# Attention, feed-forward and mixture of experts on one core: decays as float32r parts, q and k of the first pair loaded first, denser warm-up

## The chip, the core and the metric

The kernel runs on one core of one Trainium2 chip. Its engines have instruction queues of their own: TensorE (PE; its weight loads are shown apart as PEld), VectorE (DVE), ScalarE (ACT), GpSimd (POOL) and SyncE (SP, which here only issues DMAs). Each works through its queue in program order and waits on semaphores of the others. The metric is the device time of one execution in microseconds.

## The reference

Three stages follow one another, all in float32, on 2304 tokens of width 512:

```
cum = cumsum(log(clip(f, 1e-4, 1)))                    # 4 batches x 8 heads x 576
scores = q k^T / 8 + cum[i] - cum[j], causal           # "forget" attention, head size 64
attn = softmax(scores);  x = attn v                    # reshaped to 2304 x 512
h = x w_in;  g = h if h>=1, 0 if h<=-1, else (h+1)^2/4
x = g w_out                                            # 512 -> 2048 -> 512
e = argmax(normalise(x) . normalise(emb));  gate = softmax prob of e
out = gate * relu(x w1[e]) w2[e]                       # 8 experts, 512 -> 1024 -> 512
```

## The kernel before

**Attention.** The 32 heads are worked through as 16 pairs (i = 0 to 15; four pairs make a batch). Per pair, `load` fetches q and k (`rawq`, `rawk`, four DMAs each), `turned` transposes them on VectorE (`qt`, `kt`), and five units follow, c = 4, 3, 2, 1, 0: c = 4 takes the last 64 rows of both heads (576 columns, as two matmuls of 288), c < 4 a block of 128 rows against w = 128(c+1) columns for each head. A unit's scores go into one of two double banks of PSUM (`SR`, `SRx`); VectorE subtracts the mask and takes the row's extreme (L548), ScalarE takes the exponential and its sum (L553), VectorE the reciprocal (L558, L560), GpSimd scales (L564), TensorE transposes the probabilities (L578) and multiplies them with v (`X`, L618; `U`, L671).

**The decays.** `forget_rows` loads f four times, one under the other, on 4 x 32 rows, and turns it into `cum`, -8 times the running sum of the logarithms (L348 to L353). For pairs 4 to 15, the row of each head is written to memory and loaded back spread over all partitions (`cm`, `cl`), and VectorE subtracts it with the mask. For pairs 0 to 3 (`NSUM` = 4), which come before that could be there, TensorE adds it into the bank instead: `sums` multiplies a selecting column of `ident` (or a block of `pick`) with `cum`, in float32 (L514, L520). For c < 4 the two heads' sums read rows 0 to 31 and 64 to 95.

**Weights.** The kernel's wide matrix products take float32 operands as two float32r parts (high and low). Weights lie in memory as 8-byte numbers. Pieces of 128 x 512 are loaded into `war` and put together in `wax` by ScalarE and VectorE (L790 to L797), rounded to the high part on ScalarE (L801), and the low part is the difference, on GpSimd (L802). Half of the feed-forward layer's hidden columns (`half0`: 16 pieces `wa`, products `hp` and `accp`) is done between the pairs of the attention, from pair 4 on; the other half (`wb`, `hr`, `accr`) and the experts follow.

**Order.** The order on each engine is written out ahead by a planner in the kernel, the class `Order`: every step is a generator that asks for an engine with an estimated duration and a priority, and whoever is ready in the planner's time with the best priority is issued next. Loads of weights have due times in that time (`FIRST_WEIGHTS`). `keep_warm` gives TensorE small matmuls `warm` of the identity where the planner finds nothing else and the planned activity is low (`WARM`).

Of the kernel before, what the change touches and what calls it, by code (L numbers as in the profile page):

```python
# [9 lines left out]
F32 = mybir.dt.float32  # L10
# [14 lines left out]
def f32(ap):  # L25
    return ap.bitcast(F32)
# [11 lines left out]
NQK = 3  # L38
NP_ = 8
NSUM = 4  # L40
FIRST_WEIGHTS = [2000.0 + 2800.0 * n for n in range(6)] + [20000.0 + 5500.0 * n for n in range(10)]
WARM_FROM, WARM = 3000.0, 0.45


class Event:
# [149 lines left out]
def act(n, fn, prio=5.0, more=0.0):  # L195
    return Use("ACT", 155 + n / 1.2 + more, fn, prio)
# [27 lines left out]
def kernel(  # L224
# [65 lines left out]
    qz = [ap.tile([P, P], F32, name=f"qz{n}") for n in range(NQK)]  # L290

    cum = ap.tile([P, S], F32, name="cum")
    low = ap.tile([P, S], F32, name="low")
    pick = ap.tile([NH, P * NSUM], F32, name="pick")
    past = [ap.tile([P, n], F32, name=f"past{n}") for n in (512, S)]

    SR = [psa.tile([P, 2, 512], F32, name="SR"), psf.tile([P, 2, 512], F32, tag="acc", name="SRx")]
# [25 lines left out]
    def setup():  # L323
        make_identity(nc, ident)
        nc.vector.tensor_copy(pick.rearrange("p (h q) -> p h q", q=64),
                              ident[:NH, :2 * NSUM].unsqueeze(2).to_broadcast([NH, 2 * NSUM, 64]))
        for t in qz:
            nc.gpsimd.memset(t, 0.0)
        for t in past:
            nc.gpsimd.memset(t, 0.0)  # L330
        w = past[0][:, 384:]
        nc.gpsimd.affine_select(out=w, in_=w, pattern=[[-1, P]], compare_op=ALU.is_ge,
                                fill=-8e9, base=0, channel_multiplier=1)
        for j in range(2):
            w = past[1][64 * j:64 * j + 64, 512:]
            nc.gpsimd.affine_select(out=w, in_=w, pattern=[[-1, 64]], compare_op=ALU.is_ge,
                                    fill=-8e9, base=0, channel_multiplier=1)

    def forget_rows():


        def loads():
            for p0 in range(0, P, NH):
                nc.scalar.dma_start(cum[p0:p0 + NH], f.rearrange("b h s -> (b h) s"))
        yield Use("DVE", 400, lambda: (nc.vector.memset(quarter, 0.25), nc.vector.memset(low, -8.0)), 0)
        yield dma(4 * NH * S * 4, loads, 0, "ACT", k=4)
        yield Use("ACT", 1400, lambda: nc.scalar.activation(tiny, quarter, AF.Ln), 0)
        yield dve(S, lambda: nc.vector.tensor_scalar(cum, cum, 1e-4, 1.0, ALU.max, ALU.min), 0, True)  # L348
        yield act(S, lambda: nc.scalar.activation(cum, cum, AF.Ln), 0)
        go(exp_table())  # L350
        yield dve(S, lambda: nc.vector.tensor_scalar(cum, cum, -8.0, None, ALU.mult), 0, True)

        yield dve(S, lambda: nc.vector.tensor_tensor_scan(cum, low, cum, 0.0, ALU.max, ALU.add), 0)  # L353
        done(sums_there)
        yield dma(NH * S * 4, lambda: nc.sync.dma_start(rows, cum[:NH]), 2)
        done(rows_there)

    def exp_table():
        yield Use("ACT", 1400, lambda: nc.scalar.activation(tiny, quarter, AF.Exp), 0.5)
# [129 lines left out]
    def unit(i, c, started):  # L489

        yield qk_ok[i]
        heads = (None,) if c == 4 else (0, 1)
        gp_ = yield (p_b, len(heads))
        sl = yield (sr_b, ((0, 1), (2, 3)))
        bank = SR[sl[0] // 2]
        done(started)
        (qt, kt), z, _ = qkt[i]
        w = P * (c + 1) if c < 4 else S

        def scores():  # L500
            if c == 4:
                for n in range(2):
                    nc.tensor.matmul(bank[:, n, :S // 2], z, kt[:, S // 2 * n:S // 2 * (n + 1)],  # L503
                                     start=True, stop=i >= NSUM)
                return
            for j in range(2):
                p = slice(64 * j, 64 * j + 64)
                nc.tensor.matmul(bank[:, j, :w], qt[p, P * c:P * c + P], kt[p, :w],  # L508
                                 start=True, stop=i >= NSUM)

        def sums():
            if c == 4:
                for n in range(2):
                    nc.tensor.matmul(bank[:, n, :S // 2], pick[:, P * i:P * i + P],  # L514
                                     cum[:NH, S // 2 * n:S // 2 * (n + 1)], start=False, stop=True)
                return
            for j in range(2):
                p = slice(64 * j, 64 * j + NH)
                h = 64 * j + 2 * i + j
                nc.tensor.matmul(bank[:, j, :w], ident[p, h:h + 1].to_broadcast([NH, P]),  # L520
                                 cum[p, :w], start=False, stop=True)
        yield Use("PE", max(440, 1.72 * w), scores, 0.8, full=0.8)
        done(s_done[i])
        if i < NSUM:
            yield sums_there
            yield Use("PE", max(440, 1.72 * w), sums, 0.8, full=0.8)
        yield cm_ok[i, c]
        st = ap.tile([P, 8], F32, tag="st", name=f"st{i}_{c}", bufs=10)
        summed, scaled = Event(len(heads)), Event()
        left = Event(len(heads))  # L530
        for n, j in enumerate(heads):
            p = ap.tile([P, S], F32, tag="P", name=f"P{i}_{j}{c}", bufs=NP_)
            go(head(i, j, c, p, [gp_[n]], bank, st, summed, scaled, left))
        yield left
        give(sr_b, sl)
# [151 lines left out]
    def keep_warm(until):  # L687

        yield WARM_FROM
        while until.n > 0:  # L690
            g = yield (x_b, 1)
            X = psa.tile([P, 512], F32, tag="X", name=f"warm{o.seq}")
            while not x_b.waiters and until.n > 0:
                if o.slow == 2.0 or o.work < WARM * (o.now - o.window):
                    yield Use("PE", mm(P, 2), lambda: nc.tensor.matmul(
                        X[:, :P], ident, ident, start=True, stop=True), 9, after=0.0)
                else:
                    yield o.now + 150.0
            give(x_b, g)

    def attention():
        go(forget_rows())
        yield Use("POOL", 3000, setup, 0)
        go(keep_warm(xs_ok[0]))
        yield 100.0
        go(prep())
        yield sums_there
        go(loadv(0))
        for i in range(NP):
            if i + 1 < NP:  # L710
# [899 lines left out]
```

## Time and profile before

| | |
|---|---|
| median of three timed runs | 878.93 us (877.66 to 880.08) |
| the profiled execution | 878.33 us |
| its span, first to last instruction | 876.7 us |
| mean granted clock of TensorE | 0.978 |
| busy: PE, DVE, ACT, POOL | 849.6, 456.7, 360.3, 302.2 us |

The span is what the trace covers. Busy time is a sum over stages with different limits: the attention's first pairs stand in the first 80 us or so, its last in about 320, and from then on the wide matrix products fill TensorE. The granted clock is a share of full speed: 1.00 is 2.4 GHz, 0.50 is 1.2 GHz.

### The profile page before, as it was taken

The page shows a single profiled execution, that of the slowest core. Times are in us where ns is not written, and L with a number is a line of the kernel's source. Part 1 is how long each engine was busy: PE and PEld are TensorE (multiplying, and loading weights), DVE is VectorE, ACT ScalarE, POOL GpSimd, SP SyncE. Part 2 cuts the span into 40 slices and gives each one's busy share as a digit, 9 for nine tenths or more (in the row PEclk, how much of TensorE's full clock was granted, in tenths as well). Part 3 has the DMA queues.
Part 4 walks back from the last instruction along what each step waited for, and adds up shares of the span by engine and source line. Part 5 has one row for each costly group of instructions (what it writes and reads, how often), then busy time and mean ns, then how long its engine had stood idle before and what let it go on. Part 6 is the DMA issues. An engine that isn't in the chain of part 4 may idle for free.

```text
span 876.7 us, 14896 instructions
## 1 busy us (share of the span) xinstructions
PE 849.6 (97%) x5300; PEld 687.7 (78%) x5300; DVE 456.7 (52%) x1099; ACT 360.3 (41%) x838; POOL 302.2 (34%) x405
## 2 busy tenths in 40 slices
PE   7999998999999999999899999999999999999994
PEld 4655775787877789999788888888898888887684
DVE  4788778565655536676763445376643522212110
ACT  3477766655656545444533242423333212112010
POOL 2466777454654633444432122322210033000000
PEclk7699998999999999999999999999999999999998
DMA  7987756554522315343521134564431111721210
GB/s 154 143 182 173 184 141 137 127 127 116 141 66 90 93 60 135 100 134 105 196 69 49 73 120 142 162 184 150 157 121 49 49 48 49 267 94 54 92 49 25
DMA packets 153658, 100.89 MB, mean 115 GB/s; under 512 B 102724, under 2 KB 125764, under 8 KB 153584
## 3 DMA queue, kind: packets, MB, share of 16 engines
q1 hardware_dynamic: 150608, 95.43, 39.9%
q0 software_dynamic: 2784, 4.21, 1.8%
q8 instruction: 42, 0.69, 0.3%
q10 hardware_dynamic: 192, 0.30, 0.2%
q14 instruction: 32, 0.26, 0.1%
HBM read 76.33 MB, written 23.84 MB: 114 GB/s over the span
## 4 chain that ended last, share of the span: by engine, by line
PE 88%; DVE 5%; POOL 2%; DMA 2%; ACT 1%; issue 1%; SPq 0%; POOLq 0%; ACTq 0%; DVEq 0%
PE hm L847 12%; PE hr L847 11%; PE hp L847 9%; PE accp L976 8%; PE accm L984 6%; PE accr L976 6%; PE accBr L976 6%; PE accBm L984 5%; PE SR L508 5%; PE X L618 4%; PE T L578 4%; PE SR L503 2%; PE gt L1158 1%; PE U L671 1%; POOL wb L802 1%; DVE wbx L795 1%
## 5 line engine op out<-in xcount | busy, mean ns | idle before, releaser
L869 POOL TENSOR_TENSOR glr<-gr,ghr 128x512 fp32r<-128x512 f32 x36 | 46.7, 1298 | 153.3 <-PE accBr L976 73.7
L564 POOL TENSOR_SCALAR P<-P,st 128x512 f32<-128x512 f32 (+3 forms) x128 | 78.9, 629 | 48.7 <-DVE st L560 26.3
L847 PE MATMUL hr<-rx,wb 128*128 128x512 f32 (+1 forms) x384 | 89.1, 366 | 0.4 <-DVE rx L833 0.4
L847 PE MATMUL hm<-mx,wm 128*128 128x512 f32 (+1 forms) x336 | 87.4, 381 | 0.0
L553 ACT ACTIVATE P<-P,st 128x512 f32<-128x512 f32 (+3 forms) x128 | 71.5, 560 | 36.8 <-DVE st L548 35.4
L976 PE MATMUL accp<-ghp,wa 128*128 128x256 f32 x576 | 83.3, 287 | 3.2 <-DVE x_7b L1005 3.2
L976 PEld LDWEIGHTS accp<-ghp,wa 128*128 128x128 f32 x576 | 73.7, 191 | 6.7 <-DVE x_7b L1005 3.4
L878 DVE SCALAR_TENSOR_TENSOR glm<-hm,ghm 128x512 fp32r<-128x512 f32 x36 | 24.8, 690 | 103.4 <-PE accBm L984 68.6
L847 PEld LDWEIGHTS hr<-rx,wb 128*128 128x128 f32 x384 | 65.7, 188 | 13.2 <-DVE rx L833 0.8
L877 ACT ACTIVATE ghm<-hm 128x512 fp32r<-128x512 f32 x36 | 21.6, 599 | 132.6 <-PE accBm L984 111.3
L847 PEld LDWEIGHTS hm<-mx,wm 128*128 128x128 f32 x336 | 61.0, 188 | 15.7 <-issue 3.4
L869 POOL TENSOR_TENSOR glp<-gp,ghp 128x512 fp32r<-128x512 f32 x36 | 47.8, 1329 | 51.4 <-ACT ghp L868 46.8
L578 PE MATMUL T<-ident,P 128*128 128x128 f32 x320 | 55.6, 293 | 5.4 <-POOL P L564 5.0
L548 DVE CUSTOM_DVE_ANT_0 P<-SR,cm 128x512 f32<-128x512 f32 (+3 forms) x96 | 44.6, 485 | 26.7 <-PE SR L508 24.7
L578 PEld LDWEIGHTS T<-ident,P 128*128 128x128 f32 x320 | 38.2, 147 | 18.5 <-POOL P L564 8.9
L598 ACT COPY pt<-T 128x512 f32<-128x512 f32 (+2 forms) x96 | 34.8, 391 | 39.3 <-PE T L578 39.1
L863 DVE SCALAR_TENSOR_TENSOR gr<-tr 128x512 f32<-128x512 f32 x36 | 25.9, 719 | 45.7 <-POOL glr L869 27.0
L984 PE MATMUL accm<-wm,ghm 128*128 128x512 f32 x160 | 48.9, 395 | 0.0
L859 ACT ACTIVATE tr<-hr,quarter 128x512 f32<-128x512 f32 x36 | 24.8, 688 | 55.3 <-PE hr L847 25.5
L976 PE MATMUL accr<-ghr,wb 128*128 128x512 f32 (+1 forms) x160 | 47.1, 376 | 0.0
L976 PE MATMUL accBr<-ghr,wb 128*128 128x512 f32 (+1 forms) x160 | 46.6, 373 | 0.0
L976 PE MATMUL accp<-glp,wa 128*128 128x256 f32 x288 | 46.3, 283 | 0.2 <-POOL glp L869 0.2
(335 smaller groups left out, 1838.8 us busy)
## 6 DMA issues: line engine op xcount, KB each, us to landing
cm<-rows SPq DMA_DIRECT2D x24, 256.0 KB, 4.5
rawq<-in_q_dram SPq DMA_DIRECT2D x64, 72.0 KB, 3.2
rawk<-in_k_dram SPq DMA_DIRECT2D x64, 72.0 KB, 3.2
xs<-xT SPq DMA_DIRECT2D x16, 288.0 KB, 2.1
x2n<-nat SPq DMA_DIRECT2D x18, 256.0 KB, 2.3
war<-in_moe_w_in_dram SPq DMA_DIRECT2D x8, 512.0 KB, 4.6
war<-in_moe_w_out_dram SPq DMA_DIRECT2D x8, 512.0 KB, 3.5
rawv<-in_v_dram SPq DMA_DIRECT2D x32, 128.0 KB, 2.7
```

The source lines that it names most:

```text
L508: nc.tensor.matmul(bank[:, j, :w], qt[p, P * c:P * c + P], kt[p, :w], start=True, stop=i >= NSUM)
L548: yield dve(w + 80, lambda: nc.vector.tensor_tensor_reduce(out=pv_, in0=so, in1=m, scale=-0.125, scalar=3e38, op0=ALU.add, op1=ALU.min, ac ...
L553: yield act(w, lambda: nc.scalar.activation(pw, pw, AF.Exp, bias=st[:, n:n + 1], scale=-1.0, accum_out=st[:, 2 + n:3 + n]), 1, 330)
L564: yield pool1(w, lambda: nc.gpsimd.tensor_scalar(pw, pw, st[:, 6 + n:7 + n], 1.0, ALU.mult, ALU.mult), 0)
L578: nc.tensor.transpose(T[:, P * n:P * n + P], p[:, P * kb:P * kb + P], ident)
L598: yield act(n, lambda: nc.scalar.copy(dh, src), 0)
L618: nc.tensor.matmul(X[D * j:D * j + D, P * kb:], vt[:, kb, j], pt[i, j][0][:, 512 * kb:512 * kb + 512 - P * kb], start=(kb == 0), stop=(kb ...
L847: nc.tensor.matmul(oo, a[:, c, cs], x[c], start=(ip == 0 and c == 0), stop=(ip == 2 and c == KC - 1))
L863: yield dve(n, lambda: nc.vector.scalar_tensor_tensor(g, t, 0.5, t, ALU.min, ALU.mult), 2)
L869: yield pool2(n, lambda: nc.gpsimd.tensor_tensor(gl, g, f32(gh), ALU.subtract), 1)
L976: nc.tensor.matmul(acc[d][:, :w], b[:, fc, P * d:P * d + P], g, start=(fc == 0 and ip == 0 and (not narrow or d % 2 == 0)), stop=(fc == NF ...
L984: nc.tensor.matmul(acc[a], g[:, P * a:P * a + P], b[:, fc], start=(fc == 0 and ip == 0), stop=(fc == NF - 1 and ip == 2))
```

## The change

Three edits. `cum` is split for pairs 1 to 3 into three float32r parts that lie one under the other on 96 rows of `parts`: its rounding, the rounding of what is left, and the rest (`sum_parts`). The sums of these pairs are then float32r matmuls over 96 rows, with a selecting block `picks` that has the identity three times; pair 0 keeps its float32 sums. The preparation of q and k starts ahead of the setup, and the first weights are due at 6.0 instead of 2.0 us of the planner's time (later ones are moved too). The warm-up matmuls start at 1.5 instead of 3.0 us and are given up to 30 us whenever TensorE has nothing else. The planner's price of the new sums is lower, so the order moves in all engines.

```diff
-FIRST_WEIGHTS = [2000.0 + 2800.0 * n for n in range(6)] + [20000.0 + 5500.0 * n for n in range(10)]
-WARM_FROM, WARM = 3000.0, 0.45
+FIRST_WEIGHTS = [6000.0 + 2700.0 * n for n in range(5)] + [20500.0 + 5200.0 * n for n in range(11)]
+WARM_FROM, WARM = 1500.0, 0.6
...
-    pick = ap.tile([NH, P * NSUM], F32, name="pick")
+    parts = ap.tile([P, S], F32R, name="parts")
+    pick = ap.tile([NH, P], F32, name="pick")
+    picks = ap.tile([P, P * NSUM], F32R, name="picks")
...
     def setup():
...
+        for n in range(3):
+            p = slice(NH * n, NH * n + NH)
+            nc.vector.tensor_copy(
+                picks[p].rearrange("p (h q) -> p h q", q=64),
+                ident[p, NH * n:NH * n + 2 * NSUM].unsqueeze(2).to_broadcast([NH, 2 * NSUM, 64]))
...
     def forget_rows():
+        got = yield (p_b, 3)
+        low, rest, mids = (ap.tile([P, S], F32, tag="P", name=n, bufs=NP_)
+                           for n in ("low", "rest", "mids"))
+        go(sum_parts(rest, mids, got))
...
+    def sum_parts(rest, mids, got):
+        mids = mids.bitcast(F32R)
+        yield sums_there
+        yield act(S, lambda: nc.scalar.copy(parts, cum), 0.9)
+        yield dve(S, lambda: nc.vector.tensor_tensor(rest, cum, f32(parts), ALU.subtract), 0.9)
+        yield act(S, lambda: nc.scalar.copy(mids, rest), 0.9)
+        yield Use("ACT", 700, lambda: nc.scalar.copy(parts[NH:2 * NH], rest[NH:2 * NH]), 0.9)
+        yield dve(S, lambda: nc.vector.tensor_tensor(rest, rest, f32(mids), ALU.subtract), 0.9)
+        yield Use("ACT", 700, lambda: nc.scalar.copy(parts[2 * NH:3 * NH], rest[2 * NH:3 * NH]), 0.9)
+        give(p_b, got)
+        done(parts_there)
...
         def sums():
+            n3 = 3 * NH
+            if i == 0:
...
             if c == 4:
                 for n in range(2):
-                    nc.tensor.matmul(bank[:, n, :S // 2], pick[:, P * i:P * i + P],
-                                     cum[:NH, S // 2 * n:S // 2 * (n + 1)], start=False, stop=True)
+                    nc.tensor.matmul(bank[:, n, :S // 2], picks[:n3, P * i:P * i + P],
+                                     parts[:n3, S // 2 * n:S // 2 * (n + 1)], start=False, stop=True)
                 return
             for j in range(2):
-                p = slice(64 * j, 64 * j + NH)
-                h = 64 * j + 2 * i + j
-                nc.tensor.matmul(bank[:, j, :w], ident[p, h:h + 1].to_broadcast([NH, P]),
-                                 cum[p, :w], start=False, stop=True)
+                h = 64 * (2 * i + j)
+                nc.tensor.matmul(bank[:, j, :w], picks[:n3, h:h + 1].to_broadcast([n3, P]),
+                                 parts[:n3, :w], start=False, stop=True)
...
-            yield sums_there
-            yield Use("PE", max(440, 1.72 * w), sums, 0.8, full=0.8)
+            yield parts_there if i else sums_there
+            yield Use("PE", mm(w if c < 4 else S // 2, 2) if i else 1.72 * w, sums, 0.8)
...
-                if o.slow == 2.0 or o.work < WARM * (o.now - o.window):
+                if o.now < 30000.0 or o.slow == 2.0 or o.work < WARM * (o.now - o.window):
...
     def attention():
         go(forget_rows())
+        go(prep())
         yield Use("POOL", 3000, setup, 0)
         go(keep_warm(xs_ok[0]))
-        yield 100.0
-        go(prep())
```

SyncE's queue at the program's start, before (the first rows):

```order
L781 DMA war<-in_moe_w_in_dram 128x4x128
L370 DMA rawq_135<-in_q_dram 32x18x32 x4
L370 DMA rawk_144<-in_k_dram 32x18x32 x4
L781 DMA war<-in_moe_w_out_dram 128x512
L355 DMA rows<-cum 32x576
```

and of the changed kernel:

```order
L394 DMA rawq_134<-in_q_dram 32x18x32 x4
L394 DMA rawk_143<-in_k_dram 32x18x32 x4
L814 DMA war<-in_moe_w_in_dram 128x4x128
L814 DMA war<-in_moe_w_out_dram 128x512
L367 DMA rows<-cum 32x576
```

The first weights' load has moved from ahead of q to behind k.

VectorE's queue from the first work on the decays to pair 0's first reduction (`P_None`), before:

```order
L348 TENSOR_SCALAR cum<-cum 128x576
L418 STREAM_TRANSPOSE qt_128<-rawq_135 128x576
L791 TENSOR_SCALAR wax<-wax 128x512
L351 TENSOR_SCALAR cum<-cum 128x576
L418 STREAM_TRANSPOSE kt_129<-rawk_144 128x576
L353 SCALAR_TENSOR_TENSOR cum<-low,cum 128x576
L793 TENSOR_SCALAR wax<-wax 128x512
L795 SCALAR_TENSOR_TENSOR wax<-war,wax 128x512
L797 SCALAR_TENSOR_TENSOR wax<-war,wax 128x512
L548 ISA P_None_204,st_4_203<-SR,past_91 128x576
```

and of the changed kernel:

```order
L442 STREAM_TRANSPOSE qt_104<-rawq_134 128x576
L442 STREAM_TRANSPOSE kt_105<-rawk_143 128x576
L360 TENSOR_SCALAR cum<-cum 128x576
L363 TENSOR_SCALAR cum<-cum 128x576
L365 SCALAR_TENSOR_TENSOR cum<-low,cum 128x576
L824 TENSOR_SCALAR wax<-wax 128x512
L826 TENSOR_SCALAR wax<-wax 128x512
L374 TENSOR_TENSOR rest<-cum,parts 128x576
L828 SCALAR_TENSOR_TENSOR wax<-war,wax 128x512
L830 SCALAR_TENSOR_TENSOR wax<-war,wax 128x512
L582 ISA P_None_221,st_4_220<-SR,past_92 128x576
```

The transposes of q and k now stand ahead of the decays, and the first subtract of `sum_parts` (L374) stands ahead of the first reduction.

TensorE's queue from the program's start into pair 0, before:

```order
L695 MATMUL warm_127<-ident 128x128 x19
L503 MATMUL SR<-kt_129,qz_84 128x288 x2
L508 MATMUL SRx<-kt_129,qt_128 128x512 x2
L514 MATMUL SR<-cum,pick 128x288 x2
L520 MATMUL SRx<-cum,ident 128x512 x2
L508 MATMUL SR<-kt_129,qt_128 128x384 x2
L520 MATMUL SR<-cum,ident 128x384 x2
```

and of the changed kernel:

```order
L729 MATMUL warm_148<-ident 128x128 x28
L527 MATMUL SR<-kt_105,qz_84 128x288 x2
L532 MATMUL SRx<-kt_105,qt_104 128x512 x2
L540 MATMUL SR<-cum,pick 128x288 x2
L544 MATMUL SRx<-cum,ident 128x512 x2
L729 MATMUL warm_148<-ident 128x128 x5
L532 MATMUL SR<-kt_105,qt_104 128x384 x2
L729 MATMUL warm_148<-ident 128x128 x2
L544 MATMUL SR<-cum,ident 128x384 x2
```

There are more warm-up matmuls ahead of pair 0's scores, and some stand between its units. Over the whole program `warm` has 88 matmuls instead of 31.

## Rows read from the trace of the kernel before

**Rows 1.** Page of the profile: span, busy shares, granted clock in 40 slices.
```profile
span 876.7 us, 14896 instructions
...
PE 849.6 (97%) x5300; PEld 687.7 (78%) x5300; DVE 456.7 (52%) x1099; ACT 360.3 (41%) x838; POOL 302.2 (34%) x405
```

**Rows 2.** Windows: start, end, length, busy (count) by engine, clock, DMA.
```profile
17.55:35.83 18.28, 17.92 (x81) 10.84 (x79) 12.16 (x42) 10.13 (x28) 7.04 (x12) 0.50 0.85 142
36.47:80.20 43.73, 43.19 (x296) 23.57 (x294) 34.78 (x117) 31.20 (x88) 26.00 (x39) 1.00 0.88 181
40.00:60.00 20.00, 19.77 (x128) 10.11 (x127) 17.39 (x58) 14.86 (x41) 10.44 (x15) 1.00 1.00 172
```

**Rows 3.** Timeline of the start: start us, length, engine, line, work, [idle before].
```profile
0.91 0.45 SPq L781 DMA_DIRECT2D war<-in_moe_w_in_dram  x1
...
1.41 3.03 SPq L370 DMA_DIRECT2D rawq<-in_q_dram  x4
...
1.53 6.45 PE L695 MATMUL warm<-ident 128*128 128x128 f32 x38 [1.53 <-POOL ident masks.py:199]
...
5.77 2.23 SPq L370 DMA_DIRECT2D rawk<-in_k_dram  x4
5.78 0.67 ACT L790 ACTIVATE wax<-war 128x512 f32<-128x512 f32 x1 [1.48 <-DMA war<-in_moe_w_in_dram]
7.81 0.46 DVE L348 TENSOR_SCALAR cum<-cum 128x576 f32<-128x576 f32 x1 [5.16 <-DMA rawq<-in_q_dram]
...
8.31 0.68 ACT L349 ACTIVATE cum<-cum 128x576 f32<-128x576 f32 x1 [1.86 <-DVE cum L348]
...
10.75 0.78 DVE L418 STREAM_TRANSPOSE kt<-rawk 128x576 f32<-128x576 f32 x1 [0.56 <-DMA rawk<-in_k_dram]
11.46 1.32 DVE L353 TENSOR_TENSOR_SCAN cum<-low,cum 128x576 f32<-128x576 f32 x1
...
11.68 1.50 PE L503 MATMUL SR<-kt,qz 128*128 128x288 f32 x4 [3.70 <-DVE kt L418]
...
13.12 0.69 DVE L795 SCALAR_TENSOR_TENSOR wax<-war,wax 128x512 int32<-128x512 int32 x1
...
17.55 0.76 DVE L548 CUSTOM_DVE_ANT_0 P_None<-SR,past 128x576 f32<-128x576 f32 x1 [3.01 <-PE SR L514]
```

**Rows 4.** Windows of 2 us at the start, columns as in rows 2.
```profile
6.00:8.00 2.00, 1.98 (x18) 1.78 (x16) 0.19 (x1) 0.44 (x1) 0.00 (x0) 1.00 1.31 162
8.00:10.00 2.00, 0.00 (x0) 0.00 (x0) 1.58 (x4) 1.67 (x2) 0.42 (x2) 1.00 1.12 150
```

**Rows 5.** Chain of waits, pairs 0 and 3: start us, length, engine, work.
```profile
7.50 3.12 DMA rawk<-in_k_dram
...
64.96 0.97 PE SR L514 x4
...
68.82 1.06 PE SRx L520 x4
...
76.27 0.63 PE SRx L520 x4
...
77.33 0.42 PE SR L520 x4
...
83.07 0.22 PE warm L695 x2
```

**Rows 6.** Chain of waits, later layers: twelve float32r matmuls each.
```profile
205.14 1.43 PE hp L847 x12
...
447.48 2.75 PE hr L847 x12
```

**Rows 7.** Windows of 4 us after pair 3, columns as in rows 2.
```profile
84.00:88.00 4.00, 3.28 (x16) 1.66 (x18) 3.12 (x10) 2.61 (x9) 2.84 (x5) 1.00 0.75 136
140.00:144.00 4.00, 2.33 (x14) 1.58 (x13) 4.00 (x13) 2.74 (x8) 3.73 (x7) 1.00 0.56 84
144.00:148.00 4.00, 3.82 (x11) 1.46 (x13) 3.49 (x9) 2.79 (x7) 2.72 (x4) 0.70 0.94 197
```

More of the change, by code (lines that the diff above doesn't have):

```diff
@@ L292 @@
     cum = ap.tile([P, S], F32, name="cum")
-    low = ap.tile([P, S], F32, name="low")
-    pick = ap.tile([NH, P * NSUM], F32, name="pick")
+    parts = ap.tile([P, S], F32R, name="parts")
+    pick = ap.tile([NH, P], F32, name="pick")
+    picks = ap.tile([P, P * NSUM], F32R, name="picks")
     past = [ap.tile([P, n], F32, name=f"past{n}") for n in (512, S)]
@@ L303 @@
     sums_there = Event()
+    parts_there = Event()
     raw_ok = {(i, n): Event() for i in range(NP) for n in "qk"}
@@ L325, in setup @@
         nc.vector.tensor_copy(pick.rearrange("p (h q) -> p h q", q=64),
-                              ident[:NH, :2 * NSUM].unsqueeze(2).to_broadcast([NH, 2 * NSUM, 64]))
+                              ident[:NH, :2].unsqueeze(2).to_broadcast([NH, 2, 64]))
+        for n in range(3):
[3 more added lines that the diff above has]
+                ident[p, NH * n:NH * n + 2 * NSUM].unsqueeze(2).to_broadcast([NH, 2 * NSUM, 64]))
         for t in qz:
@@ L511, in sums @@
         def sums():
+            n3 = 3 * NH
+            if i == 0:
+                for n in range(2):
+                    if c == 4:
+                        nc.tensor.matmul(bank[:, n, :S // 2], pick,
+                                         cum[:NH, S // 2 * n:S // 2 * (n + 1)], start=False, stop=True)
+                    else:
+                        p = slice(64 * n, 64 * n + NH)
+                        nc.tensor.matmul(bank[:, n, :w], ident[p, 65 * n:65 * n + 1].to_broadcast(
+                            [NH, P]), cum[p, :w], start=False, stop=True)
+                return
             if c == 4:
                 for n in range(2):
-                    nc.tensor.matmul(bank[:, n, :S // 2], pick[:, P * i:P * i + P],
-                                     cum[:NH, S // 2 * n:S // 2 * (n + 1)], start=False, stop=True)
+                    nc.tensor.matmul(bank[:, n, :S // 2], picks[:n3, P * i:P * i + P],
+                                     parts[:n3, S // 2 * n:S // 2 * (n + 1)], start=False, stop=True)
                 return
             for j in range(2):
-                p = slice(64 * j, 64 * j + NH)
-                h = 64 * j + 2 * i + j
-                nc.tensor.matmul(bank[:, j, :w], ident[p, h:h + 1].to_broadcast([NH, P]),
-                                 cum[p, :w], start=False, stop=True)
+                h = 64 * (2 * i + j)
+                nc.tensor.matmul(bank[:, j, :w], picks[:n3, h:h + 1].to_broadcast([n3, P]),
+                                 parts[:n3, :w], start=False, stop=True)
         yield Use("PE", max(440, 1.72 * w), scores, 0.8, full=0.8)
```

## The prediction

> **What bounds the kernel now.** I read the page first: TensorE is busy 97% of a span of 876.7 us [rows 1], so what moves the end is work taken off TensorE, time in which it ran at half clock, or time in which it stood. Then the windows by stage. Pair 0 runs at a granted clock of 0.50, the lower of the two levels (1.2 GHz), with VectorE busy 12.16 of 18.28 us; pairs 1 to 3 run at 1.00 (2.4 GHz) with TensorE busy 43.19 of 43.73 us and VectorE 34.78 [rows 2]. So TensorE is the bound in both, in the first because it is slow. Then the timeline of the start: the weights' load goes out first, q follows, and k's four loads begin only at 5.77; k lands at 10.62 (7.50 + 3.12) [rows 3, 5]. The 38 warm-up records end at 7.98 and TensorE stands 3.70 us until k is transposed [rows 3]; in that hole it does nothing at all [rows 4], and at 17.55 the clock is at the lower level [rows 2]. Last the chain of waits, which names the pieces of TensorE's work in pairs 1 to 3 [rows 5].
>
> **Start.** The weights' load is moved behind q and k. q's four issues took 3.03 us from 1.41 on; started at 0.91 they end at 3.94. From k's first issue to its landing before: 10.62 - 5.77 = 4.85 us; so k lands at 3.94 + 4.85 = 8.8, and its transpose (0.13 later, 0.78 long [rows 3]) ends at 9.7 instead of 11.53. Bounds: nothing gained if k's first issue again stands until 5.77; 2 us more if the 512 KB that no longer run ahead shorten the landing. The weights' load now goes out after k, at about 6.2; by its old way (issued 0.91, first used 5.78) it is there at 11.1, before VectorE comes to it, so I cost it at nothing; every us beyond 13 would be paid in full, since VectorE's queue holds these steps ahead of the first softmax reduction.
>
> TensorE has 28 warm-up matmuls ahead of the scores instead of 19: 18 more records at about 0.11 us (18 records in 2.00 us [rows 4]) end at 7.98 + 2.0 = 10.0. The scores start there at the latest, 1.7 us earlier and without the hole. I take it that the clock then stays at 1.00 through pair 0.
>
> The log of f now stands behind k's transpose on VectorE: 9.7, clip 0.46, Ln 0.68, multiply 0.46 (as the clip), scan 1.32, some 0.3 for three hand-overs [rows 3]: 12.9, as before. What is new follows: the rounding of the sums on ScalarE, as long as Ln (0.68, 0.2 to hand over), 13.8; the subtract on VectorE, between 0.46 and 0.76 (the clip and the reduction of 576 elements; I take 0.76), 14.5; two weight steps of 0.69 that stand ahead, 15.9. The first reduction of pair 0 starts there instead of at 17.55 [rows 3]. TensorE needs two sums matmuls of 1 us from 12.9, so it is not late. The clip's steps on picks and pick stand in VectorE's idle start (it waits 5.16 us for its first load).
>
> **Pair 0.** From its first reduction (17.55) to the end of pair 1's k transpose (35.83) VectorE has 12.16 us of work [rows 2], plus 0.76 for the second subtract: 12.9. With TensorE at full clock VectorE is the busiest engine left. In 40 to 60 us, at full clock, it reached 17.39 of 20.00, 87% [rows 2]: 12.9 / 0.87 = 14.8, so pair 1 has its k at 30.7 instead of 35.83, **5.1 us** earlier. Bounds: at the 67% of before 19.4 us, a gain of 0.5; at 100% 12.9 us, a gain of 7.0. The new ScalarE copies (four, under 0.7 each) stand in its idle 8 us of that stretch.
>
> **Pairs 1 to 3.** The sums cost on the chain, per pair: 0.97 (288 columns twice), 1.06 (512), 0.63 (256), 0.42 (128) [rows 5], and 0.84 for 384, midway between its neighbours: 3.92. As float32r each matmul is one record instead of two. Twelve of 256 columns take 1.43 us and twelve of 512 take 2.75 [rows 6]: 0.119 and 0.229 each. Two per unit: 512 0.46, 256 0.24, 384 0.35, 288 0.27 (by columns), and for 128, which no row shows, between 0.12 and the 0.42 of before; I take 0.24, the price of 256. Together 1.56. Saved: 3 x (3.92 - 1.56) = 7.1 us.
>
> The two heads' sums of before read rows 0 to 31 and 64 to 95 and lie beside each other: 1,024 columns in 1.06 us, while the 288-column pair, both on rows 0 to 31, takes 0.97 for 576 [rows 5]. The Trainium skill, "TensorE: Matmul & The Clock Gate", section on packing small matmuls, says that matmuls on distinct row groups run at once, and that a short contraction is otherwise no cheaper than a full one. The trace agrees (1.04 against 1.68 ns a column). By it the new sums, both on the same 96 rows, can't share, as I have them; if they could, a pair would cost 0.91 and the gain be 2.0 us more.
>
> Against this stand the warm-up matmuls that the order now has between pair 1's and pair 4's first scores: 11 instead of 1, each 0.22 (a matmul is two records, [rows 5]): 2.2 us. TensorE's stretch of 43.73 can shrink by 4.9 to 38.8. VectorE's 34.78 us fill that to 90%; at its 87% they take 40.0. I take **3.7 us**, with 0 and 4.9 as bounds.
>
> **After pair 3.** Where the transformed weights and the matmuls of the first layer stand against the pairs hardly changes: the last of its 16 weight pieces stands on VectorE behind 63 softmax reductions in both orders; behind pair 15's values 924 matmuls of that layer are left instead of 912, and 24 fewer between pairs 4 and 15; at 0.119 each that is 1.4 more and 2.9 less. I count no net change, and the gain is carried to the end, TensorE being full.
>
> **Sum.** 878.33 (the profiled execution, 1.6 above its span; the three timed runs have a median of 878.93) - 5.1 - 3.7 = **869.5 us**. By the bounds 878.33 - 0.5 = 877.8 to 878.33 - 7.0 - 4.9 = 866.4.
>
> **Rivals.**
> - *The saved sums become a wait.* TensorE gets free in pairs 1 to 3, but VectorE, already 87% busy, sets the pace: 878.33 - 5.1 = 873.2. For it: in 40 to 60 us both are nearly full. Against: over the whole stretch VectorE is at 80%.
> - *The gain is given back.* The first layer's weight pieces have later due times (the sixth 20.5 us for 16.0, the last 72.5 for 69.5); if they don't come forward with the pairs, TensorE stands for them after pair 4: about 877.5. Against: the count of 63 above.
> - *More than forecast.* Both bounds reached, and the stretch after 140 us, where TensorE stood 1.67 us and then ran 3.82 us at a mean clock of 0.70 [rows 7], falls out better by 1.67 + 0.3 x 3.82 = 2.8: 863.6.
> - *Slower: the clock.* With less work in pairs 1 to 3 TensorE stands more, and the clock may fall there as it did after the hole at 8 us, or after 140 to 144 us, where it worked 2.33 of 4.00 us [rows 7]. At the lower level every us gives half: the gain of 8.8 is gone after 17.6 us; if it lasts for 26 of the stretch's 43.73 us the loss is 13 and the time 878.33 - 8.8 + 13.0 = 882.5; slower by 0.3% begins at 22.8 us. Against: 84 to 88 us, 3.28 busy of 4.00, kept 1.00, and the added warm-ups stand where the order expects holes. The Trainium skill (the same page, section on PE-mode transpose) says that transposes do not count as a busy engine for the clock; by that rule dropping the sums' share would bring this rival about. The stretch after 80 us, whose work is largely transposes, kept its clock [rows 7], so the trace does not bear it out.
>
> **How the numbers follow.** Forecast (866 to 872) 0.60; wait on VectorE (872 to 876) 0.18; more than forecast 0.08; given back 0.09; slower 0.05. The range that leaves out about 2 in 10 is 864.5 to 876.5. A change of under 0.3%, 2.6 us, can't be told from none. Faster: 0.60 + 0.18 + 0.08 = 0.86; within 0.3%: 0.09; slower 0.05.
>
> **What would show it.** k's transpose ending near 9.7 and TensorE without a hole before the scores; a granted clock of 1.00 from 12 to 36 us (a lower one there takes most of the 5.1); pair 0's first reduction near 15.9, pair 1's scores near 31; the sums' 512 pair near 0.46 us; pair 4's first scores near 71.4 (80.20 before). If these hold and the end does not move by 8 to 9 us, the carry after pair 3 was wrong; if the 128-column sums take 0.4, the 7.1 is 6.6.

## The result, and the profile after

The changed kernel takes 870.74 us (median of four runs, 869.66 to 871.74); the kernel before took 878.29 us beside it (876.23 to 880.08). The ratio is 0.9915, with a 95% interval of 0.9887 to 0.9942. Timed once more (`e12_changed_again` below) it took 870.39 us, ratio 0.9922 (0.9892 to 0.9952). So the change makes the kernel faster by some 0.8%, 7 us; 869.5 us was predicted. Of 92 runs of the kernel before that were timed beside the experiments, 25 had a mean granted clock of 0.988 or more and took 872.4 to 874.0 us, some 3 us more than the changed kernel, and the other 67 took 874.2 to 884.0 (the profiled one: clock 0.978, 878.33 us), so part of the 7 us hangs on how often the kernel before loses the clock.

The page of the changed kernel, which answers to [rows 1]:

```profile
span 870.0 us, 15066 instructions
...
PE 842.5 (97%) x5384; PEld 692.7 (80%) x5384; DVE 463.2 (53%) x1104; ACT 363.6 (42%) x842; POOL 301.6 (35%) x405
```

The span is 6.7 us shorter. TensorE has 7.1 us less busy time with 84 matmul records more: 114 warm-up records were added (176 for 62), 30 went with the float32 sums.

The timeline of its start, against [rows 3] (columns as there):

```profile
0.91 2.02 SPq L394 DMA_DIRECT2D rawq<-in_q_dram  x4
3.58 2.20 SPq L394 DMA_DIRECT2D rawk<-in_k_dram  x4
5.82 0.50 SPq L814 DMA_DIRECT2D war<-in_moe_w_in_dram  x1
8.32 0.78 DVE L442 STREAM_TRANSPOSE kt<-rawk 128x576 f32<-128x576 f32 x1 [1.06 <-DMA rawk<-in_k_dram]
9.34 1.14 PE L527 MATMUL SR<-kt,qz 128*128 128x288 f32 x4
10.69 1.36 DVE L365 TENSOR_TENSOR_SCAN cum<-low,cum 128x576 f32<-128x576 f32 x1
11.58 0.64 ACT L823 ACTIVATE wax<-war 128x512 f32<-128x512 f32 x1
12.10 0.99 PE L540 MATMUL SR<-cum,pick 32*128 32x288 f32 x3 [0.56 <-DVE cum L365]
13.06 0.75 DVE L374 TENSOR_TENSOR rest<-cum,parts 128x576 f32<-128x576 f32 x1
15.06 0.75 DVE L582 CUSTOM_DVE_ANT_0 P_None<-SR,past 128x576 f32<-128x576 f32 x1
15.73 0.75 DVE L377 TENSOR_TENSOR rest<-rest,mids 128x576 f32<-128x576 f32 x1
```

k's loads are issued 2.19 us earlier (3.58 against 5.77), its transpose ends at 9.10 instead of 11.53, and the scores follow at 9.34 without the hole of 3.70 us. The first reduction comes at 15.06 instead of 17.55. The weights' load, now behind k, is first used at 11.58 and nothing stands for it. A new hole of 0.56 us lies ahead of pair 0's sums.

Its windows by stage, against [rows 2] and, in the last three rows, [rows 7] (from pair 0's first reduction to the end of pair 1's k transpose; from pair 1's to pair 4's first scores; then single stretches):

```profile
15.06:31.35 16.29, 16.29 (x128) 12.76 (x127) 12.28 (x43) 11.32 (x30) 8.81 (x13) 0.90 0.87 165
32.27:73.90 41.63, 39.35 (x289) 24.97 (x287) 35.93 (x116) 31.49 (x88) 26.08 (x39) 1.00 0.87 176
...
84.00:88.00 4.00, 3.57 (x40) 2.49 (x38) 2.90 (x9) 3.69 (x10) 1.06 (x2) 1.00 0.96 266
136.00:140.00 4.00, 1.43 (x6) 0.50 (x6) 3.20 (x5) 2.15 (x7) 3.16 (x6) 1.00 0.77 128
140.00:144.00 4.00, 3.36 (x23) 2.42 (x24) 2.69 (x10) 3.09 (x8) 1.53 (x3) 1.00 0.32 109
```

Pair 0's stretch is 16.29 us for 18.28, pairs 1 to 3 take 41.63 for 43.73; there TensorE now stands 2.28 us (41.63 - 39.35), against 0.54 before. Pair 4's scores start at 73.90 for 80.20: the kernel is 6.3 us ahead there and ends 6.7 us ahead. Within pair 0 the clock was not at 1.00 throughout, as windows of 2 us of the same execution show:

```profile
12.00:14.00 2.00, 1.90 (x8) 1.09 (x8) 1.75 (x5) 0.94 (x3) 0.00 (x0) 1.00 0.32 72
14.00:16.00 2.00, 2.00 (x13) 1.66 (x12) 1.97 (x5) 1.95 (x4) 0.00 (x0) 0.72 0.60 135
16.00:18.00 2.00, 2.00 (x6) 0.92 (x7) 1.84 (x7) 1.74 (x4) 1.60 (x1) 0.50 0.79 165
18.00:20.00 2.00, 2.00 (x14) 1.33 (x12) 1.27 (x4) 1.72 (x5) 0.75 (x1) 0.93 0.56 88
```

The granted clock falls to the lower level (0.50) for about 3 us and returns; from 20 us on it stays at 1.00 to the end of the attention.

The new sums, and what follows each, in its timeline (pair 3 and pair 4's first scores; the answer to the sums of [rows 5]):

```profile
62.64 0.71 PE L554 MATMUL SRx<-parts,picks 96*128 96x512 f32 x2
63.34 0.33 PE L612 MATMUL T<-ident,P 128*128 128x128 f32 x1
...
69.44 0.48 PE L554 MATMUL SRx<-parts,picks 96*128 96x256 f32 x2
69.75 0.60 PE L612 MATMUL T<-ident,P 128*128 128x128 f32 x4
...
73.90 1.14 PE L527 MATMUL SR<-kt,qz 128*128 128x288 f32 x4
```

From one start to the next the 512-column pair takes 0.70 us (63.34 - 62.64), the 256-column pair 0.31.

### The profile page after: what moved, and what is told of

Its sections match the earlier page's. It is cut to its first block, busy times and chain, and to the rows that moved or that the text cites. A ratio compares the mean times of both kernels' runs of the same rounds, so it can differ in the third digit from the quotient of the medians.

```text
span 870.0 us, 15066 instructions
## 1 busy us (share of the span) xinstructions
PE 842.5 (97%) x5384; PEld 692.7 (80%) x5384; DVE 463.2 (53%) x1104; ACT 363.6 (42%) x842; POOL 301.6 (35%) x405
## 5 line engine op out<-in xcount | busy, mean ns | idle before, releaser
L598 POOL TENSOR_SCALAR P<-P,st 128x512 f32<-128x512 f32 (+3 forms) x128 | 76.6, 611 | 39.2 <-DVE st L594 25.6
L612 PE MATMUL T<-ident,P 128*128 128x128 f32 x320 | 52.4, 278 | 3.4 <-POOL P L598 2.9
L532 PE MATMUL SR<-kt,qt 64*128 64x384 f32 (+3 forms) x224 | 45.7, 485 | 4.2 <-DVE st L582 4.1
```

The source lines that it names most:

```text
L598: yield pool1(w, lambda: nc.gpsimd.tensor_scalar(pw, pw, st[:, 6 + n:7 + n], 1.0, ALU.mult, ALU.mult), 0)
L612: nc.tensor.transpose(T[:, P * n:P * n + P], p[:, P * kb:P * kb + P], ident)
```

## The experiments

The edits fall into three parts: the loads (L: q and k first, weights' due times), the warm-ups (W: from 1.5 us, whenever TensorE is free up to 30 us) and the sums (S: parts on 96 rows). The diffs below are against the changed kernel, and a part taken out is put back as it was before. "Lead" is how much earlier than in the kernel before a pair's copy of `X` (ScalarE, `xT<-X`) starts. It is read from one profiled execution of each, the kernel before's being that of 878.33 us. Kernels that ran together, on one chip, share the runs of the kernel before, whose median was 876.37 us beside e1 to e4, 876.51 beside e5 to e8 and 877.47 beside e9 to e12 (28 to 34 runs each, spread over 8 to 12 us), so ratios are compared first.

**One part or two of the three.** To take out L:

```diff
-FIRST_WEIGHTS = [6000.0 + 2700.0 * n for n in range(5)] + [20500.0 + 5200.0 * n for n in range(11)]
+FIRST_WEIGHTS = [2000.0 + 2800.0 * n for n in range(6)] + [20000.0 + 5500.0 * n for n in range(10)]
...
         go(forget_rows())
-        go(prep())
         yield Use("POOL", 3000, setup, 0)
         go(keep_warm(xs_ok[0]))
+        yield 100.0
+        go(prep())
```

To take out W:

```diff
-WARM_FROM, WARM = 1500.0, 0.6
+WARM_FROM, WARM = 3000.0, 0.45
...
-                if o.now < 30000.0 or o.slow == 2.0 or o.work < WARM * (o.now - o.window):
+                if o.slow == 2.0 or o.work < WARM * (o.now - o.window):
```

To take out S is to leave `parts`, `picks`, `sum_parts` and the new branch of `sums` out, with the planner's old price. `e1_sums_alone` is without L and W:

> Only the float32r sums of pairs 1 to 3; loads and warm-up as before. Theory A (TensorE bounds pairs 1 to 3, each 512-column pair of sums falls from 1.06 to 0.69 us): pair 4's first scores move as far ahead of pair 1's as in the changed kernel, 2.1 us, and the run takes 875 to 877 us against 878.3 before; the granted clock of pair 0 stays at 0.50. Rival B (the saved matmul time becomes a wait on VectorE, which also has the splitting to do): within 1 us of before.

`e2_loads_alone` is without W and S:

> Only q and k of pair 0 ahead of the weights, with the later due times of the weights; warm-up and sums as before. k is transposed near 9.1 us instead of 11.5. Theory A (the gain of pair 0 is the clock, and the clock fell for the hole before the scores): 17 warm-up matmuls end near 7.5, a hole of 1.6 us is left instead of 3.7; if that is short enough the clock stays up and pair 1's scores come 4 to 5 us earlier, 873 to 875 us; if it still falls, 2.4 us earlier, about 876. Rival B (the clock is of no account, since VectorE bounds pair 0): 2.4 us earlier whatever the clock, about 876.

`e3_warm_alone` is without L and S:

> Only the denser warm-up, with 32 matmuls ahead of the scores; loads and sums as before. k still comes at 11.5 us. Theory A: the warm-up runs to about 10.4, the hole shrinks from 3.7 to 1.2 us, the clock is up for most of pair 0 and pair 1's scores come 2 to 3 us earlier: 875 to 876.5 us. Rival B (VectorE bounds pair 0, the warm-up matmuls only fill TensorE): within 1 us of before.

`e4_without_sums`, without S:

> Loads and warm-up changed, the sums of all four pairs in float32 as before. Theory A: the start's gain is whole (4 us at pair 1's scores, a little more without the splitting), the 2.1 us of pairs 1 to 3 are missing: 873 to 874.5 us. Rival B (the start's gain is lost again while TensorE is full in pairs 1 to 3): 876 or more.

`e5_without_loads`, without L:

> Sums and warm-up changed, the first weights' load ahead of q and k as before. Theory A: k comes at 11.5 us, the hole is about 1.2 us, the clock up for most of pair 0; 2.4 us of the whole gain are missing: 873 us. Rival B (the order of the loads is of no account, since the decays set the start of pair 0): 871, as the changed kernel.

`e6_without_warm`, without W:

> Sums and loads changed, warm-up as before (17 matmuls ahead of the scores, few within pair 0). Theory A: a hole of about 1.6 us before the scores; the clock falls and stays low through most of pair 0, and some 2 us of the gain are missing: 873 us. Rival B (VectorE bounds pair 0 at either level of the clock): 871, as the changed kernel, or less, since no warm-up matmul is in the way.

Measured (changed kernel for comparison; clock is the mean granted from 12 to 36 us):

| | us | ratio to before (95%) | clock | lead of pairs 0, 3, 4, 15 |
|---|---|---|---|---|
| S | 878.09 | 1.002 (0.9999 to 1.004) | 0.53 | 1.3, 1.3, -6.3, -3.8 |
| L | 873.39 | 0.9979 (0.995 to 1.0009) | 0.79 | 6.4, 2.1, -3.6, -2.4 |
| W | 877.56 | 1.0012 (0.9993 to 1.0031) | 1.00 | 3.8, 4.0, -2.5, -1.3 |
| L, W | 875.67 | 0.9999 (0.9977 to 1.0021) | 1.00 | 6.4, 3.7, 3.1, 3.1 |
| S, W | 872.45 | 0.9959 (0.994 to 0.9978) | 1.00 | 6.5, 9.2, 2.0, -0.3 |
| S, L | 872.55 | 0.9961 (0.994 to 0.9982) | 0.72 | 4.4, 9.2, 6.3, 6.5 |
| S, L, W | 870.74 | 0.9915 (0.9887 to 0.9942) | 0.93 | 5.1, 5.5, 2.6, 9.5 |

No part alone, nor L and W together, can be told from no change (L comes nearest, with a median 3.0 us below); any two with S give 0.4%; all three 0.8%. The parts do not add up. A high clock alone is not the gain either: in the profiled run with W alone TensorE's clock stayed at 1.00 from 6.3 to 866.5 us, and it took 876.45 us. Clock and leads are those of the profiled executions, and that of L, at 879.80 us, lies 6.4 us above its median, so its row does not go with its time. In the profiled runs with one part, what is gained by pair 3 is lost one pair later; in the windows of the run with S alone the loss shows as TensorE standing 5.52 us in 80 to 120 us, where the changed kernel stands 0.72:

```profile
80.00:120.00 40.00, 34.48 (x258) 24.62 (x257) 32.88 (x85) 25.65 (x65) 29.86 (x42) 1.00 0.79 188
```

Each part also lets the planner write another order on every engine, so these runs price an edit together with its order. The next ones hold the order.

**The same order with float32 sums.** `e8_float32_same_order` puts the old matmuls into the new units and leaves the planner its new price, so that every engine's order is the changed kernel's, but for one small copy at the start (the parts are still made):

```diff
-                    nc.tensor.matmul(bank[:, n, :S // 2], picks[:n3, P * i:P * i + P],
-                                     parts[:n3, S // 2 * n:S // 2 * (n + 1)], start=False, stop=True)
+                    nc.tensor.matmul(bank[:, n, :S // 2], pickf[:, P * i:P * i + P],
+                                     cum[:NH, S // 2 * n:S // 2 * (n + 1)], start=False, stop=True)
...
-                nc.tensor.matmul(bank[:, j, :w], picks[:n3, h:h + 1].to_broadcast([n3, P]),
-                                 parts[:n3, :w], start=False, stop=True)
+                p = slice(64 * j, 64 * j + NH)
+                h = 64 * j + 2 * i + j
+                nc.tensor.matmul(bank[:, j, :w], ident[p, h:h + 1].to_broadcast([NH, P]),
+                                 cum[p, :w], start=False, stop=True)
```

> The changed kernel, its order and its splitting on ScalarE and VectorE kept, but the sums of pairs 1 to 3 multiplied in float32 from the rows of before. Theory A (the float32r matmuls save TensorE's time): the 512-column pair takes 1.06 us again, some 5 us of matmul time come back, of which the order's warm-up matmuls and waits take no part: 3 to 5 us slower than the changed kernel, 874 to 876. Rival B (the saving was hidden behind VectorE): within 1 us of the changed kernel.

Measured: 874.58 us, ratio 0.9987 (0.9969 to 1.0005), 3.8 us above the changed kernel's first runs and 4.6 above `e7_hole_filled` (below: the changed kernel with four more warm-ups), which was timed beside it. From pair 1's to pair 4's first scores, in its windows:

```profile
31.09:77.41 46.32, 45.74 (x319) 26.46 (x317) 36.12 (x117) 31.44 (x87) 25.43 (x40) 1.00 0.80 166
```

With float32 sums TensorE fills the stretch (45.74 of 46.32); with float32r sums the stretch is 4.69 us shorter (41.63; 5.54 in the changed kernel's second profile, 40.78) and TensorE has room in it. So more than half of the change's gain goes with the cheaper sums: by the medians of runs timed together 4.6 of 6.5 us (876.51 to 869.96), by the ratio still more, since 0.9987 can't be told from no change. The clock stayed at 1.00 over 12 to 36 us here.

**The same order without any warm-up.** `e9_same_order_no_warm`:

```diff
-                    yield Use("PE", mm(P, 2), lambda: nc.tensor.matmul(
-                        X[:, :P], ident, ident, start=True, stop=True), 9, after=0.0)
+                    yield Use("PE", mm(P, 2), lambda: None, 9, after=0.0)
```

> The changed kernel's order and arithmetic, with none of the warm-up matmuls issued, neither ahead of pair 0 nor between the stages; the rest as it is. Theory A, TensorE's clock sets the pace of the stages that wait: TensorE starts pair 0 at the low level (granted clock about 0.50 over much of 12 to 36 us, against 0.93 in the changed kernel), pair 0's xT copy comes 3 to 5 us later than in the changed kernel, and the time is 873 to 876 us. Rival B, VectorE bounds pair 0 at either level and the warm-ups between the stages only fill time in which TensorE would wait anyway: pair 0's xT copy within 1 us of the changed kernel's and the time within 1 us of it, or below by what the warm-ups themselves hold up (27.4 us of busy time of TensorE in the changed kernel).

Measured: 874.39 us, ratio 0.9965 (0.9937 to 0.9992), 4.0 us above the changed kernel beside it. First its timeline (pair 0's and pair 1's first scores, then TensorE's work from pair 4's first scores on), then its windows:

```profile
9.22 2.26 PE L527 MATMUL SR<-kt,qz 128*128 128x288 f32 x4 [9.22 <-DVE kt L442]
...
32.79 1.17 PE L527 MATMUL SR<-kt,qz 128*128 128x288 f32 x4
...
73.92 1.14 PE L527 MATMUL SR<-kt,qz 128*128 128x288 f32 x4
74.90 0.49 PE L612 MATMUL T<-ident,P 128*128 128x128 f32 x3
76.84 0.44 PE L612 MATMUL T<-ident,P 128*128 128x128 f32 x2 [1.46 <-POOL P L598]
77.47 0.44 PE L612 MATMUL T<-ident,P 128*128 128x128 f32 x2 [0.18 <-POOL P L598]
78.24 0.33 PE L612 MATMUL T<-ident,P 128*128 128x128 f32 x1 [0.34 <-POOL P L598]
79.02 0.33 PE L612 MATMUL T<-ident,P 128*128 128x128 f32 x1 [0.45 <-POOL P L598]
80.31 2.08 PE L532 MATMUL SR<-kt,qt 64*128 64x512 f32 x4 [0.96 <-DVE st L582]
```

```profile
15.85:32.67 16.82, 16.06 (x72) 8.43 (x69) 12.61 (x42) 10.40 (x29) 8.69 (x13) 1.00 0.89 166
76.00:80.00 4.00, 1.53 (x6) 0.68 (x6) 3.16 (x8) 2.14 (x6) 3.63 (x8) 0.92 1.06 226
80.00:84.00 4.00, 3.69 (x8) 1.04 (x10) 1.88 (x8) 2.26 (x5) 1.66 (x2) 0.50 0.91 135
84.00:88.00 4.00, 4.00 (x23) 1.86 (x19) 1.35 (x4) 1.45 (x4) 0.78 (x2) 0.73 0.25 88
```

Both theories are half right: the time is theory A's, but pair 0's xT copy comes only 0.3 us later than in the changed kernel's first profile and 1.0 later than in its second (`e12_changed_again` below, timed beside e9), as rival B has it. Pair 0 runs at half pace: its first four score matmuls take 2.26 us for 1.14. The clock column reads 1.00 there all the same, since the trace has no record of the clock before 31.6 us. Against the second profile, in which pair 0 ran at 1.00 throughout, pair 0's stretch is 1.67 us longer (16.82 against 15.15) and pair 4's scores start 1.93 us later (73.92 against 71.99). Against the first, which lost the clock within pair 0 for 3 us, the stretch is 0.53 us longer and pair 4's scores start together (73.92, 73.90).

More is lost behind that. Between pair 4's first scores and its next ones at 80.31 us TensorE has nothing but nine transposes of probabilities, with waits between them, where the changed kernel has warm-ups in these waits; at 79.3 us the clock falls to 0.50. Pair 2's lead is 7.6 us, as in the first profile, pair 3's 2.7, where the changed kernel has 5.5 (first profile) and 7.4 (second). A second fall follows at 140.8 us. It costs nothing beside the second profile, which has one at 136.1 us: e9 is 1.9 us behind that profile at pair 2, 4.8 at pair 3, and 4.7 from there to pair 15. So of what leaving out the warm-ups costs in these two executions, about 1.9 us are lost by pair 2, with pair 0 at half pace, and 2.8 at the fall at 79.3 us. The kernel's twelve runs lie between 870.29 and 877.37 us and the profiled one took 876.79; two took 870.29 and 870.57, as the changed kernel, and no trace shows why.

Whether the order is held or planned anew makes no difference that these runs can tell: without S 0.9987 (e8) and 0.9999 (e4), without W 0.9965 (e9) and 0.9961 (e6). So that the parts do not add up is not shown to be the planner's doing.

**A full start.** `e7_hole_filled` puts four warm-up matmuls ahead of pair 0's sums:

```diff
             if i == 0:
+                if c == 4:
+                    for n in range(4):
+                        nc.tensor.matmul(warm_x[-1][:, :P], ident, ident, start=True, stop=True)
                 for n in range(2):
...
+            warm_x.append(X)
```

> The changed kernel with four more warm-up matmuls on TensorE ahead of pair 0's first sums, where it stands 0.56 us for the scan; in the changed kernel the clock fell there for 15 to 18.6 us. If the hole is what lets the clock fall: 1.00 throughout, and at most 1 us less, 870 to 871. If it is the kind of matmul in 9 to 15 us (float32, on 32 or 64 rows), the clock falls all the same and the time is that of the changed kernel plus up to 0.4 us.

`e12_changed_again` is the changed kernel itself, and so has no diff:

> The changed kernel once more, unaltered, on the same chip as the three beside it, so that they are compared with it directly: 869.5 to 872.5 us, a ratio to the kernel before of 0.990 to 0.995. If the kernel before's own spread on this chip is what made the earlier ratio of 0.9915, the ratio is nearer to 0.996. In the profile, if the fall of the granted clock between 15.4 and 18.6 us belongs to the hole of 0.56 us ahead of pair 0's sums, it is there again; if not, the clock stays at 1.00 there with the same hole.

Measured: 869.96 us for e7, ratio 0.9937 (0.9912 to 0.9962); 870.39 for e12. The four matmuls bring nothing that these runs can tell; e7's clock stayed at 1.00 until 133.0 us. The profile of e12 says why the hole is no fixed cost; its timeline of the start, then its windows:

```profile
1.52 8.83 PE L729 MATMUL warm<-ident 128*128 128x128 f32 x56 [1.52 <-POOL ident masks.py:199]
10.19 1.14 PE L527 MATMUL SR<-kt,qz 128*128 128x288 f32 x4
```

```profile
15.14:30.29 15.15, 14.92 (x129) 11.95 (x128) 12.09 (x43) 11.21 (x30) 8.83 (x13) 1.00 0.87 163
31.21:71.99 40.78, 39.17 (x289) 24.96 (x287) 35.62 (x116) 31.32 (x88) 25.28 (x39) 1.00 0.93 183
136.00:140.00 4.00, 3.19 (x8) 1.29 (x10) 3.88 (x8) 1.68 (x5) 1.53 (x2) 0.51 0.76 174
140.00:144.00 4.00, 4.00 (x20) 2.61 (x17) 2.35 (x6) 2.38 (x6) 3.25 (x4) 0.63 0.00 0
```

Its timeline at 136 us, and that of the first profile at the same work:

```profile
136.67 2.08 PE L532 MATMUL SR<-kt,qt 64*128 64x512 f32 x4 [2.73 <-DVE st L582]
```

```profile
138.57 1.13 PE L532 MATMUL SR<-kt,qt 64*128 64x512 f32 x4 [2.73 <-DVE st L582]
```

The same 56 warm-up records take 8.83 us here and 7.98 in the first profile, the clock's first record, at 1.00, starts at 6.4 us for 4.6, the scores start later, the hole is gone and pair 0 runs at 1.00 throughout, 1.14 us shorter (15.15 against 16.29). In e8 the hole was there, 0.40 us long, and the clock did not fall. So the hole does not always cost the clock; whether it did in the first profile stays open. But e12 lost the clock at 136.1 us, in a hole of 2.73 us that the first execution has as well, without losing it. The two end within 0.6 us of each other (871.59 and 871.02).

**Sums on rows of their own.** `e10_heads_apart` leaves out the third part of the decays (a price, not a version) and with it VectorE's second subtract, and puts the two heads' two parts on rows 0 to 63 and 64 to 127, and so for the two halves of c = 4:

```diff
...
-                nc.tensor.matmul(bank[:, j, :w], picks[:n3, h:h + 1].to_broadcast([n3, P]),
-                                 parts[:n3, :w], start=False, stop=True)
+                p = slice(64 * j, 64 * j + 64)
+                nc.tensor.matmul(bank[:, j, :w], picks[p, h:h + 1].to_broadcast([64, P]),
+                                 parts[p, :w], start=False, stop=True)
```

> The changed kernel with two float32r parts instead of three (the third part of the decays is left out, so this is a price, not a version), the two heads' parts on rows 0 to 63 and 64 to 127, so that the sums of the two heads stand on different rows of TensorE. Theory A, sums on different rows lie side by side: a pair of sums of 512 columns falls from 0.64 to 0.70 us in the changed kernel to about 0.45 us, the sums of a pair of heads from 2.22 to about 1.5 us, some 2 us over pairs 1 to 3, and with VectorE's second subtraction gone too the time is 868 to 870 us. Rival B, the change-over between kinds of matmul, or VectorE, sets the pace: the pairs of sums keep 0.6 us or more from start to start, and the time stays within 1 us of the changed kernel.

`e11_heads_apart_hole_filled` is e10 with the four warm-ups of e7:

> As e10_heads_apart (the third part of the decays left out), and four more warm-up matmuls ahead of pair 0's sums, as in e7_hole_filled. Theory A, the hole ahead of pair 0's sums costs what the low clock behind it costs: granted clock 1.00 over 10 to 24 us and 0.5 to 1 us less than e10_heads_apart, 868 to 869.5 us. Rival B: pair 0 gains under 0.5 us and the planned order gives it back by pair 5: within 0.5 us of e10_heads_apart.

Measured: 870.76 us, ratio 0.9932 (0.9908 to 0.9957), and 870.05, ratio 0.993 (0.9905 to 0.9956), beside 870.39 for the changed kernel. The same unit as above in the timeline of e10, and its window from pair 1's to pair 4's first scores:

```profile
62.13 0.50 PE L556 MATMUL SRx<-parts,picks 64*128 64x512 f32 x2
62.67 0.33 PE L614 MATMUL T<-ident,P 128*128 128x128 f32 x1
```

```profile
31.20:72.86 41.66, 38.94 (x289) 23.57 (x287) 36.40 (x116) 31.54 (x88) 26.73 (x39) 1.00 0.91 181
```

The unit fell from 0.70 to 0.54 us from start to start, 1,024 columns in 0.50 us; over the five widths, medians of starts, a pair's sums cost 1.64 us for 2.20. The two matmuls of this unit start 3 ns apart; in the changed kernel they start 318 ns apart. That is 1.7 us over three pairs, and the stretch did not get shorter: 41.66 us, with TensorE standing 2.72. Theory A was right on the hardware and wrong on the time: with the sums at 2.2 us a pair, less work on TensorE no longer shortens the stretch. The four warm-ups more of e11 change nothing that these runs can tell.

What bounds it instead is not shown. VectorE is the next by busy time, 36.40 of 41.66 us (87%), but no run made its work there less. The chain of waits of e12 over the same stretch holds 32.2 us of TensorE, 3.8 of VectorE and, in one piece, 2.65 us of a load of v:

```profile
67.65 2.65 DMA rawv<-in_v_dram
```

No version ran that beats the changed kernel by more than these runs can tell.

## Why the prediction was right, step by step

- **Start: right.** k's transpose ended at 9.10 (9.7 predicted), the scan at 12.05 (12.9), the first reduction came at 15.06 (15.9). Of the scan's 0.85 us, 0.6 are k's. The scores started at 9.34 and 10.19 in two profiles (at the latest 10.0 predicted); the second is late because its warm-ups ran slowly for longer.
- **Pair 0, 5.1 us: right in size, its reason only in part.** Pair 1's k transpose ended 4.5 us earlier in one profile (31.35) and 5.5 in the other (30.29). The term rested on VectorE at 87% of the stretch; it had 12.28 of 16.29 us (75%) and 12.09 of 15.15 (80%), and the first reduction, 0.8 us earlier than forecast, made up for part of it: in part luck. That the clock "stays at 1.00 through pair 0" failed in the first profile and held in the second, at 1.1 us of difference. But without warm-ups, with TensorE at half pace, the stretch took 16.82 us, against the 18.28 of before. So of the 2.0 us by which the stretch itself shrank in the first profile (3.1 in the second) 1.5 are not the clock's: they are the new order's, or those of the 12 warm-up records, 3.18 us in all, that the kernel before ran in that stretch at half pace (at 25.41, 26.48 and 34.87 us) and e9 did not. These two were not run apart. That TensorE bounds pair 0 because it is slow was thus half of the matter. And the term is counted from an execution of before that had the clock at 0.50 from 12.5 to 36.4 us; none that kept it there was traced.
- **Sums, 1.56 us a pair: the mis-sized term.** Measured 2.20 from start to start (medians by width). The price by columns, two records at 0.119 per 256, holds for 128 columns (0.25 for 0.24) and falls short above, in the first profile: 512 take 0.64 to 0.70 for 0.46, 384 take 0.46 to 0.55 for 0.35, 288 take 0.37 to 0.41 for 0.27, 256 take 0.23 to 0.34 for 0.24. That price came from twelve matmuls in a row [rows 6]; here two stand between matmuls of other kinds. Saved were 3 x (3.92 - 2.20) = 5.2 us instead of 7.1, and e8 shows 46.32 - 41.63 = 4.7 us (5.5 against the second profile).
- **Pairs 1 to 3, 3.7 us: right in kind, too large.** 2.1 us in one profile (41.63) and 2.95 in the other (40.78). The term chose VectorE's pace, 34.78 us at 87% = 40.0, over TensorE's 38.8. VectorE was busy 35.62 of 40.78, 87%, and 35.93 of 41.63, 86%; its work was 0.8 to 1.2 us more than assumed, which gives 40.9 to 41.3 at 87%. That more savings on TensorE change nothing is shown by e10; that VectorE sets the pace is argued from its share alone. The 2.2 us set against the gain for warm-ups were no cost: without them (e9) the stretch takes 41.13 us, between the two profiles. It was luck that this error and that of the sums, 1.9 us too much saved, nearly cancel in the 4.9 us that the term gives TensorE.
- **After pair 3, no net change: right in sum, by luck, not in course.** Pair 4's scores were 6.3 us early in the first profile and 8.2 in e12, the spans ended 6.7 and 7.3 early; between, the lead went down to 2.6 (4.5) at pair 4 and up to 10.9 (10.5) at pair 9. The counts of weight pieces and matmuls that the term rests on say nothing of these swings.
- **The rival "wait on VectorE"** (873.2 us) was right in part: TensorE does stop being the limit of pairs 1 to 3 (e10), but only after a gain of 2 to 3 us, not from zero. **"Given back"** (877.5) is near the times of S and of W alone, not that of the whole; whether their weight pieces came late was not looked at. **"Slower: the clock"** did not come, in the changed kernel; e9 shows its mechanism at a smaller price: the fall at 79.3 us cost 2.8 us where 13.0 were feared. The reading set against this rival was wrong: of the 16 records of 84 to 88 us in the kernel before only 2 are transposes, the others warm-ups, scores and products with v. Where TensorE had transposes alone, in e9 ahead of 80.31 us, the clock fell, so the rule on transposes in the prediction is not refuted here.
- On the rule about row groups in the Trainium skill ("TensorE: Matmul & The Clock Gate", section on packing small matmuls): e10 agrees with it for float32r, 1,024 columns in 0.50 us on separate rows against 0.71 on the same 96. The 2.0 us that the prediction would have added by it were not to be had (1.7 saved, none of it in the time).

Open: why the runs with one part alone lose at pair 4 what they gained (only the place is shown, for S alone TensorE standing between 80 and 120 us); why the parts do not add up; what bounds pairs 1 to 3 now; and how much of pair 0's gain is the loads' and how much the order's, since no run moved the loads with the order held.

## What to carry to other kernels

Where a planner rewrites the order, take an edit out both with the order held and with a new one: held, two traces can be laid side by side; edits that could not be told from nothing alone gave 0.8% together here. A saving on the busiest engine counts only until something else sets the pace: the busy share of the next engine in its fullest stretch of before (87%) gave the new length of the stretch within 2 us here, though no run shows that this engine was the limit. Look for warm-up work where TensorE has only short pieces between waits: leaving it out cost 2.8 us at one such place, and 1.9 us up to pair 2. And profile a kernel twice: two executions of the changed one lost the clock in different places.

## What the runs showed of the hardware

- The granted clock in the profile's rows reads 1.00 also where the trace has no record of the clock, and TensorE can be at half pace there. In e9, without warm-ups, the first record starts at 31.6 us and every window from 8 to 36 us reads 1.00, yet the same four score matmuls took 2.26 us at 9.22 and 1.17 at 32.79. Early in a program the durations have to be read beside that column.
- How long the first warm-up matmuls run slowly differs between executions of the same kernel: the same 56 records took 7.98 and 8.83 us, and the first record of the clock at 1.00 starts at 4.6 and at 6.4 us.
- The same hole can cost the clock in one execution and not in another. TensorE stood 2.73 us in the changed kernel's first profile (up to 138.57 us) and the clock stayed at 1.00; it stood 2.73 us ahead of the same matmul in the second (up to 136.67) and the clock fell at 136.1. In e9 the longest wait ahead of the fall at 79.3 us was 1.46 us.
- Two float32r matmuls on separate halves of the rows overlap: in e10 two of 512 columns start 3 ns apart and take 0.50 us, where two on the same 96 rows start 318 ns apart and take 0.71.
